# LayerNorm statistics on VectorE, row maxima per head, and new work lists in a fused attention and gated MLP kernel

## The chip, the cores and the metric

The kernel runs on one core of one Trainium2 chip. The metric is the device time of one execution in microseconds (us); the kernel before took 446.6 us (median of three runs, 446.01 to 447.18). The engines are named as in the profile: PE (TensorE), DVE (VectorE), ACT (ScalarE), POOL (GpSimd), SP (SyncE, which only issues transfers here).

## The reference

Eight batches, eight heads, 576 rows of 64. First an attention whose scores below the row's maximum minus tau are dropped, then a gated MLP with a LayerNorm and a product along the rows. Cut to what matters:

```python
scores = 0.125 * q @ k.T                      # per batch and head, 576 x 576
top = max(scores, -1)
attn = where(scores >= top - 0.02, exp(scores - top), 0)
x = (attn / (sum(attn, -1) + 1e-9)) @ v        # heads side by side: 576 x 512
h = maximum(x @ w_in, 0)                      # 576 x 1024
u, v = h[:, :512], h[:, 512:]
mu, var = mean(v, -1), mean((v - mu) ** 2, -1)
v_n = (v - mu) / sqrt(var + 1e-6)             # the LayerNorm
out = (u * (w_spatial @ v_n + b_spatial[:, None])) @ w_out
```

## The kernel before

**Tiling.** A batch has four pairs of heads. A score step handles both heads of a pair for 128 rows, or the last 64 rows of two pairs together; so a batch has 18 steps, and the kernel 144. A step's scores (128 x 2 x 576, fp32) fill three PSUM banks; there are two such score buffers, so a step's matmuls wait until the step two before has been read. The rest of PSUM is two one-bank tiles `f`, shared by everything else that PE makes.

**One step, letter by letter.** `S` (scores) issues most of the matmuls; `G` (turn_bank) is a nop on POOL that waits for the first of them and releases `Y` (scores_end), the last two. `M` (top, L708) takes the negated maxima of both heads with one DVE reduction. `E` and `F` (spread) are one ACT activation for each head. For a step in `ON_ACT`, `B` (shift, L714, DVE) adds tau to the maxima, `E`/`F` (L723) apply a Prelu of huge slope, so that scores below the threshold go far below zero, and `Z` (exps, L743, ACT) takes the exponential. For the others `E`/`F` (L726) take the exponential at once, and `W` (mask, L738, DVE) zeroes what is under exp(-tau). Then `T` turns the result by a DMA transpose on SP's queue, `P` multiplies it by v on PE, and `p` divides by the row sums on DVE (L388, L390).

**Other letters.** `QA`, `QB`, `QR` turn q and k on PE, `qa`, `qb`, `qr` copy the result out of PSUM; `kd`, `sq`, `sv` are POOL copies; `RP`, `XP`, `WS` are transposes on PE. `L` and `C` load, `OUT` stores. A `d` ahead of a copy puts it on DVE instead of ACT.

**The MLP.** `v` is one 128-row chunk (five a batch) of the half that is normalized, `u` the other half, `s` the product along rows, `o` the last product; `ev`, `eu`, `es`, `eo` take their results out of PSUM. The LayerNorm of a chunk runs so:

- `ev` (ACT, L537): Relu into `vrel`, and the row sum `sm` from the accumulator
- `n` (POOL, L545): `nmean` = -sum/512
- `k` (ACT, L551): square of `vrel + nmean`, its sum `ss` from the accumulator
- `N` (POOL, L557 to L561): 1/sqrt of the variance, the shift, and the normalized chunk in bf16

**What sets the order.** `ORDER` holds four lists of such tokens, written out by hand or by a planner outside the kernel: one each for batches 0, 1 and 2, the fourth for batches 3 to 7. `name:d` stands for the work of batch "this minus d", so the MLP of a batch is done while the next batches' scores run; `-1` loads ahead. Each engine takes its instructions in the order in which the lists name them, and waits between engines follow from the data. After the lists a tail does what is left of the last two batches; its LayerNorm (last_gmlp) already takes its statistics with DVE's `bn_stats` and `bn_aggr`.

Of the kernel before, what the change touches and what calls it, by code (L numbers as in the profile page):

```python
# [8 lines left out]
F32 = mybir.dt.float32  # L9
# [7 lines left out]
    "L1:-1 L7:0 S0:0 G0:0 Y0:0 L0:-1 S1:0 M0:0 G1:0 Y1:0 QA1:0 L8:0 M1:0 E0:0 QR1:0 F0:0 B1:0 qa1:0 W0:0 "  # L17
    "S2:0 E1:0 G2:0 Y2:0 F1:0 dqr1:0 M2:0 Z1:0 S3:0 G3:0 kd1:0 Y3:0 E2:0 T00:0 QB1:0 M3:0 F2:0 qb1:0 B3:0 "
    "W2:0 F3:0 S4:0 E3:0 G4:0 Y4:0 Z3:0 M4:0 S5:0 Ci1:0 G5:0 Y5:0 sq2:0 L4:-1 QR2:0 B4:0 M5:0 Ci2:0 F4:0 "
    "QB2:0 E4:0 Cb0:0 dqb2:0 Z4:0 S6:0 T01:0 dqr2:0 B5:0 G6:0 sv0:0 Y6:0 F5:0 RP01:0 M6:0 QA2:0 E5:0 "  # L20
    "rp01:0 B6:0 qa2:0 QR3:0 E6:0 S7:0 G7:0 F6:0 Y7:0 M7:0 Z5:0 Ci0:0 S8:0 G8:0 kd2:0 L9:0 Y8:0 sq3:0 "
    "Z6:0 B7:0 M8:0 sv1:0 qr3:0 QB3:0 E7:0 RP00:0 B8:0 F7:0 kd3:0 T10:0 Cis1:0 drp00:0 E8:0 S9:0 F8:0 "
    "G9:0 Y9:0 Z8:0 M9:0 S10:0 G10:0 sq0:-1 Y10:0 Z7:0 B9:0 dqb3:0 Cis0:0 Cs1:0 M10:0 F9:0 QA3:0 L6:-1 "
    "R0:0 E9:0 dqa3:0 S11:0 B10:0 r0:0 G11:0 Cbs0:0 F10:0 Y11:0 P00:0 E10:0 M11:0 T11:0 sv2:0 Z9:0 S12:0 "
    "G12:0 sv3:0 B11:0 Y12:0 F11:0 P10:0 M12:0 Cis2:0 E11:0 Z11:0 Ci3:0 p00:0 L3:-1 p10:0 P01:0 Z10:0 "
    "Cs2:0 S13:0 p01:0 G13:0 sq1:-1 B12:0 Y13:0 F12:0 M13:0 T20:0 P11:0 E12:0 Css2:0 XP0:0 p11:0 dxp0:0 "
    "XP1:0 B13:0 E13:0 dxp1:0 QA0:-1 S14:0 F13:0 L2:-1 G14:0 Cis3:0 qa0:-1 Y14:0 L5:-1 QR0:-1 M14:0 "
    "QB0:-1 qr0:-1 Css4:0 XR0:0 Z12:0 S15:0 dqb0:-1 G15:0 F14:0 kd0:-1 Y15:0 P20:0 M15:0 E14:0 T21:0 "
# [59 lines left out]
def kernel(  # L88
# [17 lines left out]
    nc = tc.nc  # L106
# [413 lines left out]
    def moe_v(b, c):  # L520
# [10 lines left out]

        n = P if c < 4 else 64

        def ev():
            vrel = hold["vrel"] = vr.tile([P, 512], F32, name="vrel")
            sm = hold["sm"] = small.tile([P, 1], F32, name="sm")
            nc.scalar.activation(out=vrel[:n], in_=hold["t"][:n], func=ACT.Relu,  # L537
# [507 lines left out]
```

## Time and profile before

| | |
|---|---|
| median of three runs | 446.6 us |
| the profiled execution | 446.69 us, of it 444.7 us from first to last instruction (span) |
| granted TensorE clock | 0.999 |
| mean reduction L708 (128 x 1152) | 1.36 us, 144 of them |
| mean mask L738 | 1.42 us, 61 |
| mean spread L723, L726 | 0.74, 0.75 us, 288 |
| mean exponential L743 | 1.17 us, 67 for p and 16 for pr |
| mean square L551 and its read | 0.74 and 0.21 us, 35 each |
| DMA queue of SP | 95.6% of 16 engines' span |

Busy time counts overlapping instructions once, and the ends of matmuls are modelled. A mean duration reaches from an instruction's start to its end, while the next one on the same engine may have started.

### The profile page before, as it was taken

The numbers are of one execution on the slowest core, as the hardware profiler recorded it, in microseconds if no ns is written. First come the engines' busy times: TensorE is split into PE (matmuls) and PEld (weight loads), VectorE is DVE, ScalarE is ACT, GpSimd is POOL, SyncE is SP. The second block draws the span as 40 slices with busy tenths as digits, with TensorE's granted clock in tenths as the row PEclk, the third lists the DMA queues.
The fourth block names the chain that finished last, engine by engine and source line by source line (L and its number), as shares of the span: only waits on it lengthen the run. The fifth ranks groups of instructions, "written<-read, shape, count | busy, mean of one in ns | idle before, by whom it ended". The sixth has DMA issues, their size and how long they took to land.

```text
span 444.7 us, 12872 instructions
## 1 busy us (share of the span) xinstructions
PE 413.9 (93%) x5035; PEld 260.5 (59%) x5035; DVE 394.1 (89%) x615; ACT 388.5 (87%) x649; POOL 181.9 (41%) x403
## 2 busy tenths in 40 slices
PE   7676879989999899999999999999999999999995
PEld 5445556565656666666566666566665666566542
DVE  4968889899999889999999999999999999999673
ACT  3997989999989899999899998999899998999351
POOL 1256333583225734354343533455343523354031
PEclk9999999999999999999999999999999999999999
DMA  7999999899999989999999999999999997998613
GB/s 187 283 265 200 239 220 187 155 204 202 229 167 244 215 174 191 209 232 230 203 199 212 239 172 215 223 209 232 182 229 202 254 199 121 162 209 125 166 35 108
DMA packets 222556, 88.15 MB, mean 198 GB/s; under 512 B 193568, under 2 KB 218272, under 8 KB 222496
## 3 DMA queue, kind: packets, MB, share of 16 engines
q1 hardware_dynamic: 221840, 86.45, 95.6%
q8 instruction: 40, 0.66, 0.6%
q0 software_dynamic: 160, 0.52, 0.3%
q10 hardware_dynamic: 496, 0.36, 0.3%
q14 instruction: 20, 0.16, 0.2%
HBM read 32.79 MB, written 9.44 MB: 95 GB/s over the span
## 4 chain that ended last, share of the span: by engine, by line
PE 34%; DVE 25%; ACT 16%; issue 7%; DMA 3%; POOL 2%; DVEq 0%; POOLq 0%; ACTq 0%
PE s L678 14%; DVE p L738 7%; DVE s L708 6%; ACT e L726 6%; DVE negm L708 5%; PE f L605 5%; ACT e L723 5%; PE f L576 3%; PE f L329 3%; PE f L381 2%; DVE xn L390 2%; ACT p L743 2%; ACT sq L551 1%; PE f L529 1%; DMA pT<-p 1%
## 5 line engine op out<-in xcount | busy, mean ns | idle before, releaser
L678 PE MATMUL s<-qkT 64*64 64x160 f32 (+1 forms) x2304 | 172.0, 415 | 11.0 <-ACT e L723 6.4
L678 PEld LDWEIGHTS s<-qkT 64*64 64x64 f32 x2304 | 107.0, 132 | 65.8 <-ACT e L723 15.8
L723 ACT ACTIVATE e<-s,negm 128x576 f32<-128x576 f32 x166 | 115.2, 744 | 14.7 <-DVE negm L714 6.3
L708 DVE TENSOR_REDUCE s<-s 128x2 f32<-128x1152 f32 x83 | 113.1, 1363 | 12.8 <-PE s L678 10.4
L726 ACT ACTIVATE e<-s,negm 128x576 f32<-128x576 f32 x122 | 85.7, 754 | 7.4 <-DVE negm L708 7.1
L708 DVE TENSOR_REDUCE negm<-s 128x2 f32<-128x1152 f32 x61 | 82.5, 1352 | 8.6 <-PE s L678 6.6
L738 DVE SCALAR_TENSOR_TENSOR p<-e,ctau 128x1152 bf16<-128x1152 f32 x61 | 86.4, 1417 | 3.3 <-ACT e L726 3.2
L743 ACT ACTIVATE p<-e 128x1152 bf16<-128x1152 f32 x67 | 78.2, 1172 | 0.4
L215 POOL CAST v<-vl 128x512 bf16<-128x512 f32 x32 | 21.1, 660 | 72.0 <-PE s L678 71.5
L381 PE MATMUL f<-v,pT 128*128 128x65 bf16 x1008 | 44.6, 194 | 0.0
L381 PEld LDWEIGHTS <-pT 128*128 128x128 bf16 x1024 | 41.5, 98 | 2.4 <-issue 0.4
L545 POOL TENSOR_SCALAR nmean<-sm 128x1 f32<-128x1 f32 (+1 forms) x35 | 15.8, 459 | 54.9 <-PE s L678 34.4
L390 DVE TENSOR_TENSOR xn<-f,r 128x256 bf16<-128x256 f32 (+1 forms) x93 | 35.4, 381 | 2.9
L605 PE MATMUL f<-wsT,vn 128*128 128x512 bf16 x135 | 33.6, 380 | 0.0
L576 PE MATMUL f<-xT,w_in 128*128 128x512 bf16 x120 | 30.8, 380 | 0.8 <-DVE xn L390 0.7
L376 PE MATMUL f<-v,pT 128*128 128x130 bf16 x126 | 27.8, 220 | 1.9 <-DVE r L388 1.5
L192 POOL COPY qn<-ql 128x512 f32<-128x512 f32 x31 | 20.1, 649 | 21.1 <-PE s L678 20.2
L561 POOL TENSOR_SCALAR vn<-vrel,rs,nm 128x512 bf16<-128x512 f32 (+1 forms) x35 | 27.0, 771 | 3.8
L529 PE MATMUL f<-w_in,xT 128*128 128x512 bf16 x112 | 27.9, 379 | 0.3 <-ACT vrel L537 0.2
L551 ACT ACTIVATE sq<-vrel,nmean 128x512 bf16<-128x512 f32 (+1 forms) x35 | 25.8, 736 | 1.7 <-POOL nmean L545 1.5
L634 PE MATMUL f<-w_o,gT 128*128 128x512 bf16 x100 | 24.6, 379 | 1.2 <-ACT qkT L309 1.2
L341 POOL COPY qkT<-qkT 64x64 f32<-64x64 f32 x32 | 7.6, 237 | 40.5 <-PE s L678 20.2
(159 smaller groups left out, 590.5 us busy)
## 6 DMA issues: line engine op xcount, KB each, us to landing
vl<-in_v_dram SPq DMA_DIRECT2D x16, 512.0 KB, 5.3
kl<-in_k_dram SPq DMA_DIRECT2D x15, 512.0 KB, 4.6
ql<-in_q_dram SPq DMA_DIRECT2D x15, 512.0 KB, 5.0
out_dram<-oo SPq DMA_DIRECT2D x12, 512.0 KB, 4.3
uT<-in_moe_w_in_dram SPq DMA_DIRECT2D x3, 512.0 KB, 4.9
uT<-in_moe_w_spatial_dram SPq DMA_DIRECT2D x2, 576.0 KB, 4.9
vx<-in_v_dram SPq DMA_DIRECT2D x16, 64.0 KB, 3.9
pT<-p SPq DMA_TRANSPOSE x64, 6.1
```

The costliest lines, as they stand in the source:

```text
L381: nc.tensor.matmul(out=t[:, at + 65 * h:at + 65 * h + 65], lhsT=pt[:, 5 * h + j, :], rhs=vt[:, 6 * h + j, :], start=False, stop=(h == 1 an ...
L390: nc.vector.tensor_tensor(out=dst, in0=o[ps, g0:g1, 0:64], in1=r[ps, g0:g1].unsqueeze(2).broadcast_to([ps.stop - ps.start, g1 - g0, 64]), ...
L529: nc.tensor.matmul(out=t, lhsT=x_of(b, f, slice(c * P, (c + 1) * P)), rhs=w_in[:, f, 512:1024], start=(f == 0), stop=(f == 3))
L551: nc.scalar.activation(out=sq[:n], in_=hold["vrel"][:n], func=ACT.Square, bias=hold["nmean"][:n], accum_out=ss[:n])
L576: nc.tensor.matmul(out=t, lhsT=w_in[:, m, f * P:(f + 1) * P], rhs=x_of(b, m, slice(0, 512)), start=(m == 0), stop=(m == 3))
L605: nc.tensor.matmul(out=t, lhsT=vn[:, c, f * P:(f + 1) * P], rhs=wsT[:, c, 0:512], start=(c == 0), stop=(c == 4))
L678: made.append(nc.tensor.matmul(out=s_ring[g % 2][halves[k], at[h] + lo:at[h] + hi], lhsT=qks[n][halves[h], 0, m:m + 64], rhs=qks[n][halves ...
L708: nc.vector.tensor_reduce(out=nm, in_=view(s_ring[g % 2], at[0], [[at[1] - at[0], 2], [1, S]]), axis=AX.X, op=ALU.max, negate=True)
L723: nc.scalar.activation(out=e, in_=s, func=ACT.Prelu, bias=bias_, scale=scale if steps[g][1] == 4 else 1.0, alpha=1e30)
L726: nc.scalar.activation(out=e, in_=s, func=ACT.Exp, bias=bias_)
L738: nc.vector.scalar_tensor_tensor(out=numerators(g), in0=ef, scalar=ctau, in1=ef, op0=ALU.is_ge, op1=ALU.mult)
L743: nc.scalar.activation(out=numerators(g), in_=e_ring[g % 3].rearrange("p h s -> p (h s)"), func=ACT.Exp)
```

## The change

The LayerNorm can take its statistics from DVE: `bv` is `ev` without the row sum, `bs` (stats) is `bn_stats` and `bn_aggr` of `vrel`, and `N` takes mean and variance from there. `n` and `k` are not needed for such a chunk. The maxima of a step can be taken head by head: `H` for head 0, `K` for head 1. All four lists and `ON_ACT` are new; of the lists the fourth is shown. In the new lists 34 of 35 chunks use `bv` and `bs` (one in batch 1 keeps the old way), and 10, 6, 5 and 8 of 18 steps use `H` and `K`. `ON_ACT` grows from 13, 11, 9 and 10 steps to 10, 13, 11 and 12. In the tail only the count of a chunk's parts differs.

```diff
...
-    "S0:0 G0:0 Y0:0 QA1:0 M0:0 QR1:0 qa1:0 S1:0 qr1:0 G1:0 B0:0 Y1:0 W17:1 E0:0 QB1:0 F0:0 s1:2 M1:0 "
-    "qb1:0 Z0:0 S2:0 T31:1 G2:0 es1:2 Y2:0 B1:0 s3:2 M2:0 F1:0 E1:0 R1:1 sv1:0 es3:2 S3:0 B2:0 r1:1 F2:0 "
-    "L3:-1 G3:0 kd1:0 Y3:0 sq2:0 E2:0 L1:-1 s2:2 M3:0 Z1:0 sq3:0 S4:0 B3:0 es2:2 F3:0 G4:0 Y4:0 T00:0 "
-    "E3:0 o0:2 M4:0 Z2:0 P30:1 deo0:2 S5:0 B4:0 p30:1 G5:0 E4:0 Y5:0 F4:0 QA2:0 M5:0 L0:-1 P31:1 Z3:0 "
-    "S6:0 p31:1 qa2:0 G6:0 sv2:0 Y6:0 X1:1 F5:0 o1:2 M6:0 sv3:0 E5:0 o2:2 eo1:2 W5:0 T01:0 E6:0 QB2:0 "
-    "F6:0 S7:0 eo2:2 G7:0 W6:0 Y7:0 qb2:0 S8:0 Z4:0 G8:0 sv0:0 Y8:0 M7:0 L7:-1 QR2:0 s4:2 qr2:0 L4:-1 "
-    "kd2:0 v0:1 es4:2 E7:0 M8:0 v1:1 F7:0 ev0:1 W7:0 S9:0 T10:0 ev1:1 G9:0 Y9:0 F8:0 n1:1 QR3:0 o3:2 "
-    "dqr3:0 M9:0 E8:0 v2:1 k1:1 W8:0 eo3:2 S10:0 L6:-1 ev2:1 G10:0 n0:1 TR0:0 Y10:0 E9:0 P01:0 n2:1 M10:0 "
-    "kd3:0 sq0:-1 F9:0 P00:0 k0:1 S11:0 B10:0 p01:0 F10:0 T11:0 G11:0 N0:1 p00:0 Y11:0 E10:0 QB3:0 M11:0 "
-    "v3:1 qb3:0 Z10:0 W9:0 QA3:0 S12:0 OUT3:2 ev3:1 G12:0 dqa3:0 Y12:0 E11:0 OUT1:2 v4:1 M12:0 F11:0 u1:1 "
-    "ev4:1 W11:0 T20:0 S13:0 eu1:1 n4:1 G13:0 Y13:0 B12:0 N1:1 E12:0 QR0:-1 M13:0 R0:0 qr0:-1 F12:0 "
-    "QA0:-1 k2:1 S14:0 B13:0 r0:0 G14:0 F13:0 N2:1 Y14:0 dqa0:-1 E13:0 P10:0 L8:-1 M14:0 Z12:0 P11:0 "
-    "OUT4:2 n3:1 L2:-1 S15:0 p10:0 k4:1 G15:0 kd0:-1 p11:0 Y15:0 F14:0 N4:1 u4:1 M15:0 T21:0 P20:0 eu4:1 "
-    "E14:0 u0:1 p20:0 k3:1 B15:0 W14:0 u2:1 F15:0 E15:0 S16:0 deu0:1 Z13:0 G16:0 N3:1 Y16:0 deu2:1 u3:1 "
-    "M16:0 Z15:0 X0:0 QB0:-1 sq1:-1 S17:0 eu3:1 B16:0 dqb0:-1 G17:0 E16:0 TR1:0 Y17:0 s0:1 F16:0 M17:0 "
-    "Z16:0 T30:0 P21:0 es0:1 E17:0 p21:0 F17:0 L5:-1 L9:-1 ")]
+    "sv1:0 S0:0 G0:0 Y0:0 QA1:0 M0:0 QR1:0 qa1:0 S1:0 qr1:0 G1:0 B0:0 Y1:0 W17:1 E0:0 s2:2 F0:0 M1:0 Z0:0 "
+    "S2:0 G2:0 kd1:0 T31:1 Y2:0 B1:0 s1:2 es2:2 F1:0 M2:0 E1:0 QB1:0 Z1:0 S3:0 es1:2 G3:0 Y3:0 B2:0 qb1:0 "
+    "s3:2 H3:0 F2:0 L0:-1 K3:0 E2:0 R1:1 L3:-1 B3:0 es3:2 F3:0 S4:0 L1:-1 r1:1 G4:0 E3:0 sq2:0 Y4:0 s4:2 "
+    "Z2:0 H4:0 T00:0 P31:1 es4:2 Z3:0 K4:0 S5:0 p31:1 G5:0 sq3:0 Y5:0 B4:0 o0:2 F4:0 M5:0 sv2:0 E4:0 "
+    "P30:1 eo0:2 S6:0 p30:1 F5:0 G6:0 Y6:0 E5:0 X1:1 QR2:0 M6:0 QB2:0 Z4:0 S7:0 G7:0 sv3:0 dqr2:0 qb2:0 "
+    "Y7:0 TR0:0 B6:0 F6:0 o1:2 M7:0 kd2:0 E6:0 QA2:0 T01:0 eo1:2 W5:0 S8:0 qa2:0 G8:0 sv0:0 Y8:0 E7:0 "
+    "v0:1 K8:0 F7:0 H8:0 QA3:0 bv0:1 S9:0 B8:0 Z6:0 dqa3:0 OUT1:2 G9:0 Y9:0 W7:0 L4:-1 v1:1 E8:0 v2:1 "
+    "M9:0 bv1:1 o2:2 bv2:1 T10:0 bs1:1 F8:0 P01:0 deo2:2 F9:0 S10:0 p01:0 Z8:0 G10:0 Y10:0 bs0:1 u1:1 "
+    "E9:0 K10:0 L5:-1 QR3:0 H10:0 eu1:1 L7:-1 S11:0 G11:0 dqr3:0 B10:0 Y11:0 W9:0 F10:0 v3:1 E10:0 QB3:0 "
+    "M11:0 bv3:1 T11:0 S12:0 qb3:0 G12:0 N0:1 Y12:0 E11:0 P00:0 K12:0 Z10:0 o3:2 p00:0 kd3:0 bs3:1 sq0:-1 "
+    "u0:1 L2:-1 eo3:2 H12:0 L6:-1 F11:0 v4:1 N1:1 bs2:1 eu0:1 B12:0 S13:0 W11:0 bv4:1 G13:0 Y13:0 T20:0 "
+    "E12:0 u3:1 K13:0 F12:0 R0:0 sq1:-1 H13:0 eu3:1 S14:0 B13:0 r0:0 E13:0 G14:0 N3:1 Y14:0 F13:0 L9:-1 "
+    "QA0:-1 M14:0 Z12:0 u4:1 OUT4:2 S15:0 qa0:-1 B14:0 deu4:1 G15:0 N2:1 Y15:0 bs4:1 E14:0 QR0:-1 P11:0 "
+    "K15:0 qr0:-1 F14:0 T21:0 P10:0 H15:0 F15:0 S16:0 p11:0 Z13:0 G16:0 N4:1 p10:0 Y16:0 u2:1 M16:0 E15:0 "
+    "Z14:0 QB0:-1 TR1:0 kd0:-1 S17:0 B16:0 W15:0 eu2:1 G17:0 Y17:0 qb0:-1 X0:0 P20:0 F16:0 K17:0 s0:1 "
+    "E16:0 p20:0 H17:0 T30:0 F17:0 P21:0 Z16:0 es0:1 p21:0 E17:0 L8:-1 OUT3:2 ")]
 LAST = "W17:1 T31:1"
-ON_ACT = [(1, 3, 4, 5, 6, 7, 8, 9, 10, 11, 12, 13, 15), (0, 1, 3, 4, 6, 9, 10, 12, 13, 14, 15), (0, 1, 2, 3, 4, 8, 13, 15, 16), (0, 1, 2, 3, 4, 10, 12, 13, 15, 16)]
+ON_ACT = [(1, 3, 4, 6, 8, 10, 12, 13, 15, 16), (0, 2, 3, 4, 6, 8, 10, 11, 12, 13, 14, 15, 16), (0, 1, 3, 4, 7, 8, 10, 12, 13, 15, 16), (0, 1, 2, 3, 4, 6, 8, 10, 12, 13, 14, 16)]
 
 
 @with_exitstack
@@ -531,14 +531,23 @@
 
         n = P if c < 4 else 64
 
-        def ev():
+        def ev(sums=True):
             vrel = hold["vrel"] = vr.tile([P, 512], F32, name="vrel")
-            sm = hold["sm"] = small.tile([P, 1], F32, name="sm")
-            nc.scalar.activation(out=vrel[:n], in_=hold["t"][:n], func=ACT.Relu,
-                                 accum_out=sm[:n])
+            if sums:
+                sm = hold["sm"] = small.tile([P, 1], F32, name="sm")
+                nc.scalar.activation(out=vrel[:n], in_=hold["t"][:n], func=ACT.Relu,
+                                     accum_out=sm[:n])
+            else:
+                nc.scalar.activation(out=vrel[:n], in_=hold["t"][:n], func=ACT.Relu)
             if c == 4 and b:
                 o = hold["o"] = orr.tile([P, 512], F32, name="o")
                 nc.scalar.copy(out=o[64:128], in_=hold["t"][64:128])
+
+        def stats():
+            st = small.tile([P, 6], F32, name="st")
+            mv = hold["mv"] = small.tile([P, 2], F32, name="mv")
+            nc.vector.bn_stats(out=st[:n], in_=hold["vrel"][:n])
+            nc.vector.bn_aggr(out=mv[:n], in_=st[:n])
 
         def mean():
             nmean = hold["nmean"] = small.tile([P, 1], F32, name="nmean")
@@ -554,17 +563,26 @@
         def norm():
             rs = small.tile([P, 1], F32, name="rs")
             nm = small.tile([P, 1], F32, name="nm")
-            nc.gpsimd.tensor_scalar(out=rs[:n], in0=hold["ss"][:n], scalar1=1.0 / 512,
-                                    scalar2=1e-6, op0=ALU.mult, op1=ALU.add)
+            if "mv" in hold:
+                nc.gpsimd.tensor_scalar(out=rs[:n], in0=hold["mv"][:n, 1:2], scalar1=1.0,
+                                        scalar2=1e-6, op0=ALU.mult, op1=ALU.add)
+            else:
+                nc.gpsimd.tensor_scalar(out=rs[:n], in0=hold["ss"][:n], scalar1=1.0 / 512,
+                                        scalar2=1e-6, op0=ALU.mult, op1=ALU.add)
             nc.gpsimd.tensor_tensor(out=rs[:n], in0=rs[:n], in1=mhalf[:n], op=ALU.pow)
-            nc.gpsimd.tensor_tensor(out=nm[:n], in0=hold["nmean"][:n], in1=rs[:n], op=ALU.mult)
+            if "mv" in hold:
+                nc.gpsimd.tensor_scalar(out=nm[:n], in0=hold["mv"][:n, 0:1], scalar1=rs[:n],
+                                        scalar2=-1.0, op0=ALU.mult, op1=ALU.mult)
+            else:
+                nc.gpsimd.tensor_tensor(out=nm[:n], in0=hold["nmean"][:n], in1=rs[:n],
+                                        op=ALU.mult)
             nc.gpsimd.tensor_scalar(out=vn_ring[b % 2][:n, c, :], in0=hold["vrel"][:n],
                                     scalar1=rs[:n], scalar2=nm[:n], op0=ALU.mult, op1=ALU.add)
 
         def send():
             if b:
                 nc.sync.dma_start(out=out[b - 1, 512:576, :], in_=hold["o"][64:128])
-        return "act", mm, ev, mean, square, norm, send
+        return "act", mm, ev, mean, square, norm, send, stats
 
     def moe_u(b, f):
         hold = {}
@@ -699,13 +717,17 @@
 
     negm = {}
 
-    def top(g):
+    def top(g, heads=slice(0, 2)):
 
         if on_act(g):
             nm = s_ring[g % 2][:, 704:706]
+        elif g in negm:
+            nm = negm[g]
         else:
             nm = negm[g] = small.tile([P, 2], F32, name="negm")
-        nc.vector.tensor_reduce(out=nm, in_=view(s_ring[g % 2], at[0], [[at[1] - at[0], 2], [1, S]]), axis=AX.X,
+        h0, n = heads.start, heads.stop - heads.start
+        dims = [[at[1] - at[0], n], [1, S]] if n > 1 else [[1, S]]
+        nc.vector.tensor_reduce(out=nm[:, heads], in_=view(s_ring[g % 2], at[h0], dims), axis=AX.X,
                                 op=ALU.max, negate=True)
 
     def shift(g):
@@ -894,17 +916,18 @@
         if (name, b) in done or b < 0:
             return
         kind = name.rstrip("0123456789")
-        a = [int(x) for x in name[len(kind):]] if kind not in "SGYMBEFZW" else []
-        g = 18 * b + int(name[len(kind):]) if kind in "SGYMBEFZW" else 0
+        a = [int(x) for x in name[len(kind):]] if kind not in "SGYMHKBEFZW" else []
+        g = 18 * b + int(name[len(kind):]) if kind in "SGYMHKBEFZW" else 0
         if b >= B or g >= len(steps):
             return
         if kind in ("B", "Z", "W") and on_act(g) == (kind == "W"):
             return
         i = 4 * b + a[0] if a else 0
         m = 2 * b + a[0] if a else 0
-        if kind in "SGYMEFBZW":
+        if kind in "SGYMHKEFBZW":
             {"S": scores, "G": turn_bank, "Y": scores_end, "M": top, "E": lambda g: spread(g, 0),
-             "F": lambda g: spread(g, 1), "B": shift, "Z": exps, "W": mask}[kind](g)
+             "F": lambda g: spread(g, 1), "H": lambda g: top(g, slice(0, 1)),
+             "K": lambda g: top(g, slice(1, 2)), "B": shift, "Z": exps, "W": mask}[kind](g)
         elif kind in ("QA", "QB", "qa", "qb"):
             task("q", i, kind[1] in "Bb")[1 + (kind[0] == "q")]()
         elif kind in ("QR", "qr", "kd"):
@@ -933,6 +956,10 @@
             chores[kind[:2]][len(kind) == 3](a[0])
         elif kind == "OUT":
             task("o", b, a[0])[3]() if a[0] < 4 else task("v", b + 1, 4)[6]()
+        elif kind == "bv":
+            task("v", b, a[0])[2](False)
+        elif kind == "bs":
+            task("v", b, a[0])[7]()
         elif kind in ("n", "k", "N"):
             task("v", b, a[0])[3 + "nkN".index(kind)]()
         else:
@@ -983,7 +1010,7 @@
                 for d in due:
                     d()
                 due.clear()
-                if f[0] == "act" and len(f) == 7:
+                if f[0] == "act" and len(f) == 8:
                     f[3]()
                     f[6]()
                     due.extend(f[4:6])
```

## The prediction

> **What bounds the kernel now.** I read the page's busy table first, then windows over the eight batches, the chain of waits in a repeated batch, the waits by engine, and last the timeline, for what an instruction really occupies.
>
> ```profile
> PE 413.9 (93%) x5035; PEld 260.5 (59%) x5035; DVE 394.1 (89%) x615; ACT 388.5 (87%) x649; POOL 181.9 (41%) x403
> ...
> core 0: us, PE busy (x) PEld busy (x) DVE busy (x) ACT busy (x) POOL busy (x), PEclk, DMA share, GB/s
> 8.07:28.00 19.93, 14.34 (x167) 9.12 (x167) 15.78 (x20) 16.64 (x24) 5.34 (x14) 1.00 1.08 252
> 28.00:52.00 24.00, 18.07 (x276) 13.03 (x278) 18.93 (x36) 20.53 (x30) 14.87 (x31) 1.00 1.04 225
> ...
> 179.18:229.54 50.36, 49.86 (x620) 31.38 (x616) 47.66 (x70) 47.42 (x82) 21.90 (x49) 1.00 1.06 215
> ```
>
> No engine alone is the bound: three are within six points. Batch 0 (8 to about 52 us) has the most air: in its two windows ACT works 37.2 of 43.9 us, DVE 34.7. The repeated batches (179 to 381 us, about 50.4 each) have 47.7 of DVE, 47.4 of ACT and a PE that looks full.
>
> ```profile
> 236.87 1.33 DVE p L738
> 238.20 1.31 DVE s L708
> ...
> 255.46 1.13 PE s L678 x12
> 256.59 0.97 PE f L576 x4
> 257.56 0.44 PE f L329 x4
> ```
>
> Inside a repeated batch the chain lies on DVE from 235.2 to 254.4 us, with short breaks, and on PE from 254.4 to 269.8; around these it goes back and forth between DVE and ACT. So time is won only where an engine's own work in such a stretch shrinks, or a hand-over between engines gets shorter.
>
> ```profile
> 265.01 1.36 DVE L708 TENSOR_REDUCE s<-s 128x2 f32<-128x1152 f32 x1
> 266.28 0.68 DVE L619 TENSOR_TENSOR gT<-f,uT 128x512 bf16<-128x512 f32 x1
> ...
> 423.17 0.69 DVE L784 BATCH_NORM_STATS2 st<-vrel 128x6 f32<-128x512 f32 x1 [0.73 <-ACT vrel L782]
> 423.90 0.18 DVE L786 BATCH_NORM_AGGREGATE mv<-st 128x2 f32<-128x6 f32 x1
> ```
>
> ```profile
> 248.10 0.73 ACT L551 ACTIVATE sq<-vrel,nmean 128x512 bf16<-128x512 f32 x1
> 248.71 0.21 ACT L551 ACTIVATION_READ_ACCUMULATOR sq<-vrel,nmean 128x1 f32 x1
> 248.80 1.38 ACT L723 ACTIVATE e<-s,negm 128x576 f32<-128x576 f32 x2
> ```
>
> Columns are start, duration, instruction. Neighbours overlap, so I price by slots, from one start to the next on the same engine. A reduction holds DVE for 1.27 us, not 1.36; square and accumulator read hold ACT for 0.70 (248.10 to 248.80), not 0.94. From the same timeline: mask (L738) 1.33, shift (L714) 0.07, a 512-wide PSUM eviction 0.60 on DVE and 0.48 on ACT, one spread (L723, L726) 0.63, exponential (L743) 1.06, Relu with its read 0.57 and without about 0.48; on PE a step of scores 1.13.
>
> **What the Trainium skill says.** "Perfetto Trace Analysis", section Optimizing Scalar/DVE Operations, puts the fixed cost of a DVE operation on PSUM near 125 ns of engine time; here the reduction's slot is 1.27 for 1152 elements, and at the 0.96 GHz that the page "VectorE: DVE Perf Modes" (Specifications) gives, 1.20 of it is elements, so 0.07 is left. The same section of the first page says that splitting instructions can help where an engine makes bubbles elsewhere without being saturated; DVE at 89% is only just that. Its section Identifying the Most-Contended Engine warns that PE's busy share misleads; the trace agrees, since the PE slots of a repeated batch add up to 47.8 (below), not to the 49.9 shown. Its section What "DMA-bound" means counts a solid issuing queue as a bound; SP's queue issues for about 45 of the 50.75 us from 229.54. I found no page with a price for the statistics operation; the tail of before shows it.
>
> **The change part by part.** Counts are those of the built programs.
>
> 1. *Statistics, 34 of 35 chunks.* ACT loses square and read (0.70) and the Relu's read (0.57 to 0.48): 0.79 x 34 = 26.9 us. DVE gains statistics and aggregate: 0.73 from start to start, and 0.11 for the aggregate if an independent instruction follows, 0.84 x 34 = 28.6. POOL loses L545, 0.46 x 34 = 15.6, and with it these waits:
>
> ```profile
> POOL nmean L545 <- PE s L678: 34.4, 11, 8.1
> POOL nmean L545 <- ACT vrel L537: 20.5, 8, 3.4
> ```
>
> POOL was idle then anyway, but everything behind stands in its queue: the nop of a step's bank turn (G), which releases the last two score matmuls. In batch 2 this was on the chain: 145.1 to 153.8 us run through square, L557 to L561 and L545. The new wait is DVE's aggregate on its own statistics, and POOL's L557 form on the aggregate; in the repeated list one to three score steps lie between bs and N, so I cost it at nothing. If DVE is late, POOL stands still, and every G behind it.
>
> 2. *Steps on ACT, 83 to 94.* Eleven masks leave DVE, eleven shifts come: 11 x (1.33 - 0.07) = 13.9 off; ACT gains 11 x 1.06 = 11.7.
>
> 3. *Maxima per head, 61 steps.* Two reductions of 576 for one of 1152. Not in the trace; by the 0.07 above each costs 0.67 and a split adds 0.07 (4.3 in all), by the page's 125 ns about 0.125 (7.6), by durations up to 0.15 (9). I take 0.07. The gain is on the hand-over: where the step is not on ACT, the first spread starts after one half, 0.64 earlier (half of 1.27). Where it is, the shift needs both halves, and only an early start on head 0 is won, 0.2 at most by my estimate (head 0 is complete before the last two, 160-wide, of a step's eight matmuls, which are about a seventh of its 1.13). At least the added DVE time is lost, if the early start is hidden.
>
> 4. *Evictions.* DVE loses about 12 to 13 us (ten wide uT, ten qkT, less five narrow uT), ACT gains about 11.
>
> Sum: DVE +6, ACT -4, PE 0. The work has not become less; it is shifted to DVE. By list, slots summed over every token (us; without the tail):
>
> list (batch): PE | DVE before, after | ACT before, after
> first (0): 30.3 | 37.1, 39.6 | 39.2, 37.7
> second (1): 43.6 | 45.1, 45.9 | 47.6, 47.3
> third (2): 48.3 | 46.5, 47.6 | 46.5, 45.4
> fourth (3 to 7): 47.8 | 46.7, 47.0 | 45.7, 45.4
>
> Since the bound moves, I also cut each list into stretches of three score steps, took the most loaded of PE, DVE and ACT in each, and added up (mean of the three places to cut): first list 42.2 to 41.8, second 49.6 to 49.7, third 50.3 to 51.5, fourth 49.1 to 49.5. By work alone the new lists are 0.1 to 1.2 us longer per batch after batch 0, 2.9 in all.
>
> Against it stand the hand-overs. *Batch 0* takes 44 where its work is 39.2: a score buffer's round trip is 1.13 + 1.36 + 1.37 and its signals, some 4.4 us for two buffers, 2.2 a step, and that is the pace seen. Ten of its steps are split, three of them not on ACT: (3 x 0.64 + 7 x 0.2) / 2 = 1.7 at most, as two steps share a trip. I take 1.0 off (0 to 1.7). *Batch 1*: 0. *Batch 2*: of the 8.7 us through POOL, L545 (1.5) and the wait for squares go, the work adds 1.2: 0.5 off (1.5 off to 1.2 on). *Each repeated batch* lies 1.3 above its stretch sum, 50.4 to 49.1. Its eight splits, two not on ACT, shorten trips by (2 x 0.64 + 6 x 0.2) / 2 = 1.2 at most; masks come one step in two or more (not on ACT: 5, 7, 9, 11, 15, 17, instead of 5 to 9 in a row), so DVE's long stretch is broken up; POOL's queue is freer. I take 0.8 off for these, 0.4 on for work: 0.4 off, times five is 2.0 (1.2 off to 1.0 on each, so 6 off to 5 on). *Tail* (from 414): same code, 0. Total 1.0 + 0.5 + 2.0 = 3.5 off. The profiled execution took 446.69, its span 444.7, so 2.0 lie outside; 441.2 + 2.0 = 443.2, and its median over runs was 446.6, the same within 0.1. I say 443.
>
> What is late next: with hand-overs shorter, PE and DVE at 47 to 48 of 50, then SP's queue. No batch can go under 47.8, so not much over 2.6 x 6 = 16 us can be had there.
>
> **Rivals.** (a) *Nothing is left*: shorter hand-overs are paid back by DVE's added work; 446 within 1.3. For it: the sums of DVE and ACT together hardly change. Against: the lists are wholly different, and a hit within 0.3% would be luck. (b) *VectorE becomes the bound, slower*: the statistics stand in DVE's queue ahead of maxima. Place: steps 9 to 13 of the fourth list, where four statistics lie and the three steps from S9 have DVE 10.3 against PE 9.0. From the point where no other engine has slack to take it, each 0.84 delays a maximum, so a spread, so the next scores; if half of the five pass through, 2.1 a batch, less the 0.8 above, 1.3 x 6 = 8 on: 454. Splits at 0.125 would add another 0.4 a batch. For it: DVE already carries the chain for 19 us of a batch. Against: two masks less per batch. (c) *SP's queue*: transposes and loads are issued in a new order; before shows single waits of 5.0 us (pT at 126.6) and 3.9 (kl at 168.4) on the chain. One such wait of 2 to 3 us per repeated batch gives 10 to 15 on: about 458. For it: the queue is nearly solid. Against: the eight transposes of p keep nearly the same steps. (d) *The change isn't what it says*: built counts show 34 statistics, 61 splits and 94 steps, so no.
>
> **How the numbers follow.** Chances: forecast (faster) 0.50, (a) 0.13, (b) 0.28, (c) 0.09. A measurement of this kernel tells about 0.3% (1.3 us) from no change, so faster 0.50, same 0.13, slower 0.37. If the forecast holds, 437 to 445; with (b) reached to its own price, and the gains of every part at their full size at the other end (1.7 + 1.5 + 6 = 9, so 437.5, and a little more where ACT's relief counts), the range is 436 to 454.
>
> **What would show it.** Right: batch 0 shorter by about 1 us; the repeated period near 50.0; DVE busy near 400, ACT near 384; statistics near 0.69 and halves near 0.75 long; no POOL on the chain in batch 2; fewer waits of scores for L723's line. Wrong: a repeated period over 50.7 with ACT waiting for maxima behind statistics, which is (b), or with PE waiting for pT or loads, which is (c); or halves of 0.85 and more.

## The result and the profile after

The changed kernel took 467.94 us (median of four runs, 465.49 to 469.23), the kernel before 446.39 beside it: a ratio of 1.0474 (95% interval 1.0425 to 1.0523). It is slower, and outside the range of 436 to 454. Among the runs of one kernel the time is longer where the mean granted clock of TensorE was lower (the changed kernel: 465.49 us at 0.998, 469.23 at 0.990), so a few us between two medians may be the clock's; the periods of repeated batches below were read where the clock was 1.00, unless another stands beside them. The engines' busy times on the page came out near the forecast:

```profile
PE 414.1 (89%) x4985; PEld 260.6 (56%) x5035; DVE 404.1 (87%) x726; ACT 385.6 (83%) x576; POOL 167.6 (36%) x369
```

DVE was expected near 400, ACT near 384. But PE worked 413.9 us of a span of 444.7 before, and 414.1 of 463.7 now: of the 19.0 us of longer span 18.8 are idle time of PE. So PE did not get more work; it waited longer. Windows over two repeated batches say the same (columns: span, then busy time and count of PE, PEld, DVE, ACT, POOL, then clock, DMA share, GB/s):

```profile
204.67:257.95 53.28, 50.04 (x613) 31.50 (x623) 48.41 (x87) 47.49 (x71) 19.71 (x44) 1.00 1.03 203
257.95:311.24 53.29, 50.05 (x613) 31.49 (x623) 48.42 (x87) 47.50 (x71) 20.02 (x44) 1.00 1.00 195
```

A repeated batch takes 53.3 us in place of 50.4, with DVE's and ACT's busy time up by less than 0.8. Below, a period is the time from the first spread of a batch to the first of the next, read from the timeline of ACT. By three steps of a repeated batch:

```
steps          0-2   3-5   6-8   9-11  12-14  15-17  period
before         7.7   7.4   9.6   9.0   7.5    9.2    50.4
after          7.6   8.3   8.3   11.5  8.1    9.4    53.3
```

By batch, periods were 47.5, 51.3, 53.1 and four times 50.4 (one of them 50.7) before, and are 48.3, 51.9, 55.2 and four times 53.1 to 53.3 after; the last batch, up to its last spread, took 48.0 and takes 50.5. The rest is the tail. What ended PE's waits is in the groups of instructions, first of the kernel before, then of the one after (at the end of a row: idle time before the group, and by what it ended):

```profile
L678 PE MATMUL s<-qkT 64*64 64x160 f32 x1152 | 132.7, 308 | 11.0 <-ACT e L723 6.4 <-ACT e L726 1.8 <-DVE negm L714 1.2
L723 ACT ACTIVATE e<-s,negm 128x576 f32<-128x576 f32 x166 | 115.2, 744 | 14.7 <-DVE negm L714 6.3 <-DVE r L388 6.0 <-PE f L462 1.5
```

```profile
L696 PE MATMUL s<-qkT 64*64 64x160 f32 x1152 | 133.0, 309 | 28.0 <-ACT e L748 12.4 <-ACT e L745 11.4 <-POOLq L711 2.8
L745 ACT ACTIVATE e<-s,negm 128x576 f32<-128x576 f32 x188 | 131.6, 746 | 19.4 <-DVE negm L736 15.4 <-DVE r L388 3.4 <-PE s L696 0.2
```

The 160-wide matmuls are the first and the last of a step. They wait 28.0 us in place of 11.0. Of these, 23.8 are waits of a step's first matmul for spreads on ACT (L745, L748, formerly L723, L726) that have not freed the score buffer; only 2.8 are waits of the last ones for the bank turn (L711). The spreads in turn wait 15.4 us in place of 6.3 for DVE's shift. Not one engine is full: the round from maxima to spreads to the next scores became longer. The chain of waits of the changed kernel at steps 10 to 12 of a repeated batch shows one such place:

```profile
244.25 0.44 PE s L696 x4
244.73 0.18 DVE r L388
244.94 0.42 DVE xn L390
245.36 0.61 DVE st L549
246.03 0.07 issue
246.09 0.76 DVE s L730
246.88 0.77 DVE s L730
...
247.75 0.16 DVE negm L736
247.93 1.38 ACT e L745 x2
249.36 0.51 PE s L696 x4
...
250.12 0.20 POOL rs L567
250.40 0.55 POOL rs L572
...
255.87 0.49 PE s L696 x4
```

The scores ended near 244.7, but their maxima started at 246.09, behind a division and one of the statistics (st); then come two halves, shift, spreads, and the next scores. From 250.12 POOL works through one normalization, copies of q and k, and a second normalization, and only then comes the next bank turn, for which the scores waited until 255.87.

### The profile page after: what moved, and what is told of

It is laid out like the page before. It is cut to its first block, busy times and chain, and to the rows that moved or that the text cites. A ratio compares the mean times of both kernels' runs of the same rounds, so it can differ in the third digit from the quotient of the medians.

```text
span 463.7 us, 12902 instructions
## 1 busy us (share of the span) xinstructions
PE 414.1 (89%) x4985; PEld 260.6 (56%) x5035; DVE 404.1 (87%) x726; ACT 385.6 (83%) x576; POOL 167.6 (36%) x369
## 4 chain that ended last, share of the span: by engine, by line
PE 26%; DVE 25%; ACT 14%; issue 7%; POOL 5%; DMA 4%; POOLq 0%; DVEq 0%; ACTq 0%
PE s L696 11%; DVE s L730 10%; ACT e L745 4%; ACT e L748 4%; DVE negm L730 3%; DMA pT<-p 3%; PE f L529 3%; PE f L652 2%; ACT p L765 2%; PE f L623 2%; DVE xn L390 2%; DVE p L760 2%; PE f L381 2%; DVE st L549 2%; ACT pr L765 2%
## 5 line engine op out<-in xcount | busy, mean ns | idle before, releaser
L696 PE MATMUL s<-qkT 64*64 64x160 f32 (+1 forms) x2304 | 174.8, 415 | 28.0 <-ACT e L748 12.4
L730 DVE TENSOR_REDUCE s<-s 128x1 f32<-128x576 f32 (+1 forms) x138 | 135.1, 979 | 22.5 <-PE s L696 17.9
L696 PEld LDWEIGHTS s<-qkT 64*64 64x64 f32 x2304 | 105.7, 131 | 81.0 <-ACT e L745 22.0
L745 ACT ACTIVATE e<-s,negm 128x576 f32<-128x576 f32 x188 | 131.6, 746 | 19.4 <-DVE negm L736 15.4
L765 ACT ACTIVATE p<-e 128x1152 bf16<-128x1152 f32 x78 | 90.1, 1164 | 0.5
L748 ACT ACTIVATE e<-s,negm 128x576 f32<-128x576 f32 x100 | 72.2, 751 | 17.7 <-DVE negm L730 7.7
L730 DVE TENSOR_REDUCE negm<-s 128x1 f32<-128x576 f32 (+1 forms) x67 | 69.1, 1045 | 4.1 <-PE s L696 3.7
L760 DVE SCALAR_TENSOR_TENSOR p<-e,ctau 128x1152 bf16<-128x1152 f32 x50 | 71.2, 1424 | 1.5 <-ACT e L748 1.4
L215 POOL CAST v<-vl 128x512 bf16<-128x512 f32 x32 | 24.0, 750 | 51.1 <-PE s L696 50.2
L567 POOL TENSOR_SCALAR rs<-mv 128x1 f32<-128x1 f32 (+1 forms) x34 | 7.4, 217 | 66.9 <-PE s L696 58.2
L311 ACT COPY qkT<-f 128x512 f32<-128x512 f32 (+1 forms) x50 | 22.9, 457 | 1.6 <-PE f L348 1.1
```

Of the source, the lines that this page charges most:

```text
L696: made.append(nc.tensor.matmul(out=s_ring[g % 2][halves[k], at[h] + lo:at[h] + hi], lhsT=qks[n][halves[h], 0, m:m + 64], rhs=qks[n][halves ...
L730: nc.vector.tensor_reduce(out=nm[:, heads], in_=view(s_ring[g % 2], at[h0], dims), axis=AX.X, op=ALU.max, negate=True)
L745: nc.scalar.activation(out=e, in_=s, func=ACT.Prelu, bias=bias_, scale=scale if steps[g][1] == 4 else 1.0, alpha=1e30)
L748: nc.scalar.activation(out=e, in_=s, func=ACT.Exp, bias=bias_)
L760: nc.vector.scalar_tensor_tensor(out=numerators(g), in0=ef, scalar=ctau, in1=ef, op0=ALU.is_ge, op1=ALU.mult)
L765: nc.scalar.activation(out=numerators(g), in_=e_ring[g % 3].rearrange("p h s -> p (h s)"), func=ACT.Exp)
```

## The experiments

Each run was timed beside the kernel before, whose median was 446.25 to 447.27 in the five comparisons. Ratios carry 95% intervals. Line numbers of variants differ by some ten, since their lists are set in shorter lines.

**1. One part of the change at a time, on the old lists.** Statistics alone (before_stats), with the new tokens where the old ones stood:

```diff
-ev0:1 ... n0:1 ... k0:1      (all chunks)
+bv0:1 ...      ... bs0:1
```

> The lists of before, with the statistics on VectorE alone: ev becomes bv, k becomes bs at the same place, n is left out. If statistics on VectorE are the cause, about 460 (0.84 us a chunk on an engine that carries the chain for a part of each batch, less what ACT wins). If order or halves are the cause, 444 to 450.

468.44 us, ratio 1.0499 (1.0481 to 1.0516), period 53.8. DVE is busy for 51.2 us of that period, ACT for 44.0, and the chain of waits runs through DVE, statistics and maxima one behind the other:

```profile
243.47 1.26 DVE negm L740
244.74 0.61 DVE st L559
245.37 0.18 DVE mv L560
245.55 1.30 DVE p L770
246.86 1.28 DVE s L740
248.13 0.60 DVE st L559
...
256.03 1.37 DVE s L740
257.40 0.60 DVE st L559
258.02 0.18 DVE mv L560
```

All five statistics of the batch lie on that chain (the other two at 261.50 and 264.64), together 3.6 us; the period grew by 3.4.

Halves alone (before_split), in as many and the same steps as in the changed kernel:

```diff
-M3:0
+H3:0 K3:0      (10, 6, 5 and 8 steps of the four lists)
```

> The lists of before, with the maxima head by head in the same steps of each list as in the change (10, 6, 5 and 8), H then K at the place of M. If halves are the cause, 455 to 462 (61 steps, 0.2 us or more of each on the way to the shift). If the order is the cause, 446 to 450: some 0.07 to 0.15 us a split.

451.96 us, 1.013 (1.0114 to 1.0145): 5.4 us slower, where their own added slots were put at 4.3. On balance no hand-over gained anything. The changed kernel's timeline of DVE shows one reason:

```profile
225.32 1.57 DVE L730 TENSOR_REDUCE s<-s 128x1 f32<-128x576 f32 x2 [0.48 <-PE s L696]
226.92 0.16 DVE L736 TENSOR_SCALAR negm<-s 128x2 f32<-128x2 f32 x1
...
261.96 1.40 DVE L730 TENSOR_REDUCE negm<-s 128x1 f32<-128x576 f32 x2
...
271.22 1.37 DVE L730 TENSOR_REDUCE s<-s 128x2 f32<-128x1152 f32 x1 [0.47 <-PE s L696]
272.62 0.16 DVE L736 TENSOR_SCALAR negm<-s 128x2 f32<-128x2 f32 x1
```

For a step on ACT (output `s`) the shift starts 1.40 us after one whole reduction (271.22 to 272.62), but 1.60 after the first of two halves (225.32 to 226.92): there the second half starts when the first has ended (246.09 and 246.88 in the chain above), and the shift needs both. In a step not on ACT (output `negm`) the halves overlap and take 1.40 together. Of the fourth list's eight split steps six are on ACT, in this run too.

The sets of steps alone (before_onact), with one reduction and the old sums, and all three parts on the old lists (before_all):

```diff
-ON_ACT = [..., (0, 1, 2, 3, 4, 10, 12, 13, 15, 16)]
+ON_ACT = [..., (0, 1, 2, 3, 4, 6, 8, 10, 12, 13, 14, 16)]
```

> Before's lists, one maximum for both heads, sums on ScalarE, but the sets of score steps on ScalarE of the changed kernel (94 in place of 83). VectorE loses 11 masks and gets 11 shifts (13.9 us less of slots), ScalarE gets 11 exponentials (11.7 us more), and nothing else moves. Theory of bursts (the new list's order and ScalarE's share cost what statistics and splits don't): the lists were ordered for the old sets, so 447 to 455. Theory that work on VectorE alone decides: 440 to 445. With it the parts on the old lists can be added: 446.5, + 22 for statistics, + 5.4 for splits, + this one's difference, against 480.9 for all three together.

> The lists of before with all three parts of the change: statistics on VectorE at the place of the square, halves in the same steps as in the change, and the change's steps on ACT (a mask made an exponential at the mask's place, and the reverse). If the new order itself costs nothing or helps, this is at 472 to 480, above the changed kernel (467.9), as statistics alone took 468.4 and halves alone added 5. If the new order is a cause of its own, it is below 466.

470.88 (1.0543, 1.0521 to 1.0564) and 480.88 (1.0762, 1.0731 to 1.0794). 22, 5.4 and 24.4 do not add up to the 34 of all three together. The period shows where: statistics alone add 3.4 us to it, halves 0.8, the sets 2.7, all three 4.5, so that on top of the other two the sets cost only 0.3. That ACT was full (49.2 us busy of a period of 53.1 in before_onact) is at most a part of the sets' price: with no sums on any engine they still cost 1.8 a batch (part 5). In both runs batch 0 also grew, by 6.6 and 7.5 us, while the granted clock there was 0.91 (1.00 before); how much of that is the clock's was not tested. The new lists win back 13 of these 34, not all.

**2. One part taken back, on the new lists.** After_no_split puts both heads' maxima back in one reduction at the first one's place; after_no_stats gives the normalization a constant for mean and variance, so that the 34 statistics are left out; after_old_stats brings the sums on ACT and POOL back.

```diff
-H3:0 ... K3:0
+M3:0                                   (after_no_split)
-nc.vector.bn_stats(out=st[:n], in_=hold["vrel"][:n])
-nc.vector.bn_aggr(out=mv[:n], in_=st[:n])
+hold["mv"] = mvc                       (after_no_stats: a constant tile)
-bv0:1 ... bs0:1
+ev0:1 ... n0:1 k0:1                    (after_old_stats)
```

> The changed kernel with every pair H, K made one reduction M again, at the place of the first of the two; the rest of the lists as changed. If the halves are the cause (a shift now waits for two halves one behind the other), most of the 21 us come back: 450 to 456. If the statistics on VectorE or the order of the lists is the cause, 465 to 470.

> The changed kernel without the two statistics instructions in the loop: N takes a constant in place of mean and variance, so this leaves the LayerNorm's statistics out; all else stays. If the statistics on VectorE are the main cause, it is below 446 (28 us of VectorE gone): 438 to 448. If the order of the lists is the cause, 458 or more.

> The changed kernel with the LayerNorm's statistics as before: Relu with its sum, nmean on POOL and the square on ACT at the place where bs stood. If the statistics in front of maxima on VectorE are the cause, 450 to 457. If halves or order are the cause, 467 or more (ACT gets 0.8 us a chunk back, 27 us in all, and POOL waits for sums).

463.12 (1.0363, 1.031 to 1.0416), 459.92 (1.0287, 1.0248 to 1.0326) and 510.38 (1.1432, 1.1409 to 1.1454). The first two give 4.8 and 8.0 us back, but steps 9 to 11 stay at 11.7 and 11.1. So neither alone explains that place. The third says little of the statistics' price: the new order asks for mean and square as early as DVE could have them, and 29.9 us of waits of the square for POOL's mean are added.

**3. Where the statistics and GpSimd's work stand in the fourth list.** After_bs_late puts the statistics behind the maxima of steps 10, 12 and 15; after_pool puts the copies of q and k and the second normalization behind the bank turn of step 13.

```diff
-v1:1 ... bs1:1 ... bs0:1 u1:1 E9:0 K10:0 ... H10:0
+v1:1 ... u1:1 E9:0 K10:0 ... H10:0 bs1:1 bs0:1      (after_bs_late, one of three places)
-kd3:0 bs3:1 sq0:-1 ... N1:1 bs2:1 ... S13:0 ... G13:0 Y13:0
+kd3:0 bs3:1 ... bs2:1 ... S13:0 ... G13:0 Y13:0 sq0:-1 N1:1      (after_pool)
```

> The changed kernel, in the fourth list alone each bs moved behind the next maxima (bs1 and bs0 after H10, bs3 and bs2 after H12, bs4 after H15). If statistics hurt by standing ahead of maxima, 1 to 2 us a batch come back in five batches: 458 to 463. If their time on VectorE hurts wherever they stand, or POOL then waits longer for them, 466 or more.

> The changed kernel, in the fourth list alone the POOL work sq0 and N1 moved from ahead of G13 to behind Y13, so that the bank's turn does not stand behind 3 us of copies and normalization. If that queue is a cause, 0.7 us and more a batch come back: 460 to 464. If it has slack, 467 to 469.

470.26 (1.0543, 1.0497 to 1.059) and 466.35 (1.0434, 1.0382 to 1.0485). With the statistics late the period rises to 54.2. They no longer stand ahead of step 10's maxima, but they now stand between these and the shift:

```profile
247.66 0.68 DVE L561 BATCH_NORM_STATS2 st<-vrel 128x6 f32<-128x512 f32 x1
...
249.44 0.15 DVE L748 TENSOR_SCALAR negm<-s 128x2 f32<-128x2 f32 x1
```

The maxima ended at 247.75 and the spread started at 249.63, 1.9 us later; in the changed kernel 0.3 us lie between them (247.64 to 247.93). So a statistic costs on either side of the maxima. POOL's first normalization still started only when the scores let the bank turn go (251.82), not later for the statistics. With POOL freed the period stays at 53.2 and steps 9 to 11 at 11.5, so POOL's queue alone does not hold this place; that DVE's holds it as well is read from the chain, not tested.

**4. The kernels without statistics and halves.** Before_lean and after_lean leave the statistics out (a constant in their place; in after_lean one chunk of batch 1 keeps its old sums) and take both heads' maxima in one reduction. The two differ in order, sets of steps and the engine of some evictions.

> The kernel before with its statistics left out on every engine (mean and variance are constants; no row sum, no square on ScalarE, no mean on GpSimd), lists, sets and merged maxima as before. It shows the most that taking the sums off ScalarE and GpSimd can bring on the old lists (ScalarE 27 us less work, GpSimd 16). Theory that ScalarE's sums were hidden beside VectorE and TensorE: 444 to 447, no batch period under 50. Rival, that they held up the pace: 436 to 441, periods near 49. The difference from the run of the old lists with statistics on VectorE (468.4) is the price of 34 statistics there.

> The changed kernel with its maxima merged again (H and K gone, both heads in M at the first one's place) and its statistics left out (mean and variance are constants). What is left over the kernel before is the new order and the new sets of steps alone, with some 20 us less work for VectorE than before had. Theory that statistics and splits add up (8 and 5 given back alone): about 455. Rival, that each of them alone is hidden behind the other (VectorE is the only bound): 440 to 447. Steps 9 to 11 of the repeated batch at 11 us in the first case, at 9.5 or under in the second.

Before_lean: 444.6 us, 0.9966 (0.9947 to 0.9985). After_lean: 457.73, 1.0247 (1.0221 to 1.0272). So taking all sums off ACT and POOL is worth 1.9 us on the old lists, and the new lists cost 13.1 us by themselves, though DVE and ACT have room. The windows of a repeated batch, before_lean first:

```profile
212.69:263.10 50.41, 49.56 (x613) 31.39 (x616) 47.66 (x71) 44.08 (x66) 20.54 (x44) 1.00 1.02 210
```

```profile
218.31:270.67 52.36, 50.19 (x613) 31.42 (x616) 44.26 (x69) 47.83 (x71) 20.42 (x44) 1.00 1.03 205
```

The sum of DVE and ACT is the same to 0.4, and yet the period is 2.0 longer; steps 9 to 11 take 11.7 here too. The chain of waits of after_lean there, with POOL between the scores of two steps for 6 us:

```profile
248.06 0.20 POOL rs L575
...
249.34 0.77 POOL vn L587
250.17 0.24 POOL qkT L352
250.47 0.61 POOL qn L203
251.07 0.55 POOL kn L203
251.72 1.21 POOL rs L575
...
254.02 0.49 PE s L704 x4
```

**5. Sets or order?** Both kernels without statistics, with each other's sets of steps on ACT. A mask takes the place of an exponential and the reverse, and a new shift stands right behind its maxima; other places for these were not tried.

> The kernel before without statistics (444.6) with the changed kernel's sets of steps on ScalarE. ScalarE has room for them now (27 us of sums are gone, 11.7 of exponentials come), so that, unlike in the run with the sums kept (470.9), no engine is overloaded. If the sets cost by themselves: 452 to 462. If they cost only where ScalarE was full: 444 to 449, and the 13 us between the two kernels without statistics are the order's.

> The changed kernel with merged maxima and without statistics (457.7) with the sets of steps of the kernel before, masks placed where the list had exponentials and the other way round. If the order costs whatever the sets: 456 to 462. If the sets are the cause: 445 to 450.

```
median us, no statistics   old sets   new sets
old order                  444.6      464.2
new order                  472.8      457.7
```

Ratios of the crossed ones: 1.0401 (1.0383 to 1.042) and 1.0603 (1.058 to 1.0625). Both came out slower than either guess: each order is better with its own sets, and crossing them costs 15 to 20 us although no engine is busy for more than 46.3 us, besides PE's 50.1, of a repeated period of 52.4 and 53.4. Of the 19.6 us on the old order 6.4 lie in batch 0, at a granted clock of 0.91 there (1.00 without the new sets), so a part may be the clock's; the repeated batches, at 1.00, still lose 1.3 to 2.0 each. The 13 us can't be divided between order and sets.

**6. What in the new order?** After_lean_spread puts POOL's first normalization behind step 11's bank turn, the second behind step 12's, the copies behind step 13's. After_lean_both also moves v4 and its eviction to step 14; after_both is the same two moves on the changed kernel. After_even moves two chunks of the output product from steps 9 and 12 to 6 and 8, after_even_no_split the same with one reduction.

```diff
-G12:0 N0:1 Y12:0 ... kd3:0 bs3:1 sq0:-1 ... v4:1 N1:1 bs2:1 eu0:1 B12:0 S13:0 W11:0 bv4:1 G13:0 Y13:0
+G11:0 ... Y11:0 N0:1 ... G12:0 Y12:0 N1:1 ... v4:1 ... S13:0 W11:0 bv4:1 G13:0 Y13:0 sq0:-1      (spread)
+... S14:0 ... G14:0 N3:1 Y14:0 v4:1 F13:0 bv4:1                                              (both)
-v2:1 M9:0 bv1:1 o2:2 ... deo2:2 ... Z10:0 o3:2 ... eo3:2
+E5:0 o2:2 X1:1 QR2:0 M6:0 deo2:2 QB2:0 ... E7:0 o3:2 eo3:2                                   (even)
```

> The changed kernel with merged maxima and without statistics (457.7), where GpSimd's two normalizations and the copies of q and k, that all stand between the bank turns of steps 12 and 13 in the fourth list, are spread: the first goes behind step 11's turn, the second behind step 12's, the copies behind step 13's. Theory that GpSimd's queue stretches steps 12 to 13: 0.5 to 1.5 us a batch back, 450 to 455. Rival, that TensorE's own queue (v4, o3, u0 and P between these scores) holds them: 457 to 459.

> The run before, and the fifth normalized chunk (v4 and its eviction) moved from step 12 to step 14, so that TensorE has 0.97 us less between the scores of steps 12 and 13. If TensorE's queue there holds the pace: another 0.5 to 1 us a batch back, 447 to 453. If the order costs nothing at this place and is lost all over the list: 456 to 459.

> The changed kernel itself, maxima per head and statistics as they are, with both moves (GpSimd's work spread over the turns of steps 11 to 13, v4 in step 14). If the order at this place is what is left beside statistics and splits: as much back as the two runs without statistics show, 458 to 464. If VectorE's queue takes over as soon as TensorE and GpSimd are freed: 466 or more.

> The changed kernel, where the fourth list's third and fourth output chunks of the decoder MLP (o2, o3 with their evictions) are moved from steps 9 and 12 to steps 6 and 8, so that TensorE has 0.9 us less in each of steps 9 and 12; work and engines as they were. Theory of the burst (TensorE's queue in steps 9 to 12 holds back the next scores): 1 to 2 us a batch come back, 458 to 463, and steps 9 to 11 go from 11.5 to 10.5 or less. Rival (VectorE's queue holds them, whatever TensorE does): 467 or more.

> The run with the decoder MLP's chunks moved, with its maxima merged again too. If burst and splits act apart: the run with the chunks moved less about 5 us, so 453 to 458 in the burst theory, 462 or more in the rival's.

Spread: 455.6 (1.0204, 1.0188 to 1.0221), 2.1 us less. Both: 458.8 (1.0273, 1.0258 to 1.0289): steps 9 to 11 fall from 11.7 to 9.9, but steps 12 to 14 rise from 6.4 to 9.0. After_both: 467.43 (1.0466, 1.0449 to 1.0483), period 53.1 in place of 53.3, no gain that can be told from the spread. Even: 481.43 (1.077, 1.0723 to 1.0816): steps 9 to 11 fall from 11.5 to 10.1, and steps 3 to 8 and 12 to 14 lose 5.3 together in the three repeated batches where the granted clock was 0.97, 3.7 in the one where it was 1.00. Its variant with one reduction: 475.84 (1.0658, 1.0621 to 1.0696), 5.6 less; but a batch at a clock of 1.00 took 55.3 to 55.7 there and 55.6 in even, so these 5.6 are not the price of the halves. So the place that stands out can be relieved, and the time comes back next to it. The theory of a burst on PE alone falls; POOL's queue is worth some 2 us.

No run beat the kernel before, apart from before_lean, which leaves the statistics out; it bounds what any cheaper statistics could win on these lists at 0.34% (0.15 to 0.53).

## Why the prediction was wrong

With the parts taken off one after the other (medians of 467.9, 463.1, 457.7, 444.6 and 446.5), the 21.4 us are: halves 4.8, statistics on DVE 5.4, the new order with its sets 13.1, and the old sums 1.9 off. Taken in another order, statistics are 8.0 and halves 2.2. These medians mix clocks. By repeated periods at a clock of 1.00, halves are worth 0.4 to 0.7 us with the statistics (53.3 against 52.6 to 52.9), 0.1 at most without them (52.4 both times), and the new lists 2.0 (52.4 against 50.4), so that the lists remain the largest part.

*Right.* The counts and slots: statistics 0.69 us, busy times of DVE and ACT within about 4. No POOL on the chain in batch 2. And the place named in rival (b): steps 9 to 11 of the repeated list, with a period over 50.7. Its mechanism, ACT waiting for maxima behind statistics, is on the chain there, but it is not what makes these steps long: without the statistics they still take 11.1 of 11.5.

*Wrong: the hand-over gains (the step "I take 0.8 off for these", and 1.0 in batch 0).* This is the step that failed. The work summed by stretches of three steps was 49.1 before and 49.5 after, and what lay above it was taken as 1.3, less gains. Measured, with the same sums worked out for the variants from the prediction's slots:

```
kernel             sum by stretches   period   above
before             49.1               50.4     1.3
before_lean        48.7               50.4     1.7
before_stats       52.1               53.8     1.7
before_onact       50.9               53.1     2.2
before_lean_sets   49.3               52.2     2.9
after_lean_spread  49.0               51.8     2.8
after_lean         49.0               52.4     3.4
after_lean_sets    49.9               53.4     3.5
after              49.5               53.3     3.8
after_lean_both    48.8               52.7     3.9
after_even         50.0               57.0     7.0
```

The 57.0 of after_even is at a clock of 0.97; its batch at 1.00 took 55.6, which is 5.6 above. Where the order stays the old one and the statistics are added, the sum is good: 49.1 to 52.1 forecasts the period of before_stats to 0.4. For another order or other sets it says nothing: what lies above ranges from 1.3 to 5.6. The prediction took the new order's loss in hand-overs to be the old one's, and only looked for reasons to make it smaller. 2.5 us more were lost in each, some 12 over the five repeated batches, where 2 to gain were forecast. Batch 0, forecast 1.0 shorter, became 0.8 longer.

The traces show that the forecast gains themselves were not there. For a step not on ACT the first spread was to start after one half, 0.64 us earlier. In 16 of 17 such steps of the changed kernel, and in all 17 of before_split, it started only after both had ended, even where ACT was idle. After the halves that started at 261.96 above:

```profile
263.46 0.74 ACT L748 ACTIVATE e<-s,negm 128x576 f32<-128x576 f32 x1 [0.82 <-DVE r L388]
```

The two halves had ended at 263.36. The one exception, step 11 of batch 2, is the only one whose list names a spread between its two halves; there it started 0.06 us after the first. Both halves write into one tile, so most likely a spread waits for every write to that tile that the list names before it; lists with the spread between the halves elsewhere were not tried. For the steps on ACT the early start on head 0 did not come either: in no split step did the first half start before the last matmul of its scores (the earliest 0.34 us after that matmul's start), and in 42 of 61 the new lists take head 1 first, whose scores end last.

*Wrong: maxima per head.* 0.07 a split was too low: DVE's busy time grew by 7.4 us in before_split (394.1 to 401.5), 0.12 a split, close to the 0.125 that the prediction had worked out and not taken; the end time grew by 5.4. And the 1.2 us off per batch are not there. "Only an early start on head 0 is won" also left out that the second half starts after the first has ended, so that a split step on ACT reaches its shift 0.2 us later than a whole one. The Trainium skill ("Perfetto Trace Analysis", section Optimizing Scalar/DVE Operations) says that breaking up instructions may help where DVE is not saturated and makes bubbles elsewhere; this trace, with DVE at 87 to 89%, shows a loss in both orders.

*Wrong: the worth of part 1.* In before_lean 24.0 us of busy time left ACT and 12.5 left POOL (the prediction's slots say 26.9 and 15.6), and the end time fell by 1.9: nearly all of it was hidden beside DVE and PE. On the old lists the statistics (35 there; by 0.84 some 29 us) cost 23.8, the distance from before_lean to before_stats: four fifths of their work pass through. With the new lists they cost 5.4 to 8.0, most likely since masks have left DVE; but these lists cost 13.1 themselves, so that of the 16 to 18 us saved 3 to 5 are left.

*Rival (b)* had the price nearly right (8 us for the statistics), but it too took the hand-overs as otherwise unchanged, hence 454. "I cost it at nothing" for POOL's new wait on DVE holds: on the chain shown POOL waits for scores, not for statistics, and with later statistics (after_bs_late) only the last normalization of a batch waits longer, 1.0 us in place of 0.6.

*Rival (c)* showed once, in batch 2. On SP's queue a transpose of p was issued behind a load and two stores, and landed 8.17 us later, which the chain shows as one piece (in the timeline: start, duration of the issue):

```profile
155.49 0.53 SPq L168 DMA_DIRECT2D vl<-in_v_dram  x1
156.12 0.55 SPq L584 DMA_DIRECT2D out_dram<-o  x1
156.86 1.16 SPq L671 DMA_DIRECT2D out_dram<-oo  x1
158.12 4.55 SPq L771 DMA_TRANSPOSE pT<-p  x1
```

That batch is 2.1 us longer than before; its last three steps take 14.1 in every run with the new lists (16.7 in after_old_stats), 11.9 before, and 10.5 in before_lean and before_stats, where POOL's mean is gone from this place, as the prediction had it. No run moved this load or these stores, so the cause is read from the trace only.

*Open.* Which hand-overs of the new order make up the 13 us beyond the 2 of POOL's queue was not found: two further moves (v4, and the output chunks) only shifted the loss to the steps beside them. The tail, from the last spread on, was forecast unchanged and is 1.7 longer (33.1 in place of 31.4); in after_no_stats and after_lean it is 31.5 and 31.7, so on the new lists it is seen only with the statistics. Why was not tried.

## What to carry to other kernels

Before pricing a move of work between two engines, time two cuts: the work left out altogether (what its removal can bring, here 1.9 us) and the work added to its new engine with nothing else changed (here 23.8). Where lists are ordered by hand or by a planner, a sum of busy slots priced added work in the same order well here, and another order not at all; put the hand-over loss of a new order into the range as an unknown of several times the old one. Before counting a gain for a split instruction, look in a trace whether the consumer starts on the first part and whether the parts overlap; here it did so in one step of 17.

## What was not expected of the hardware

Two half reductions that write into the score tile ran one behind the other (1.54 to 1.57 us for both, in all 30 pairs that follow each other directly in the changed kernel), two that write into a tile of their own overlapped (1.40 to 1.42, 13 pairs). A crossing of order and sets of steps, with every engine's work within its room, cost 15 to 20 us. On POOL the same operation on 128 x 1 elements (rs) took 0.20 us and, one batch turn later, 1.21 on the chain of after_lean; spans on POOL are rough, and no run tells what stretched it. The granted clock was 0.998 in the changed kernel's profiled run, and 0.962 in the longest of the runs (after_old_stats), whose PE was busy for 85% of its span. With the same list for batch 0, that batch took 48.3 us in the changed kernel at a clock of 1.00, 49.8 in after_pool at 0.94 and 50.0 in after_both at 0.93.
